# Two layers of cached attention and a token mixer on one core: a third PSUM bank keeps rows of V between the layers, and sums of heads go into the columns of x

## The chip, the cores and the metric

The kernel runs on one core of one Trainium2 chip. The metric is the time of one execution on the device in microseconds (us), as the median of several runs; the profile shows one execution, with its trace.

## What is computed

Two tokens (batch B = 2, one new position each) of width D = 512 pass four steps, each added to its input: attention over a cache, a token mixer, and both once more with the same weights and the same cache.

```python
x = x + _A_ref(_layernorm(x), k_cache, v_cache, wq, wo)   # layer 0
x = x + _B_ref(_layernorm(x), w1, b1, w2, b2)
x = x + _A_ref(_layernorm(x), k_cache, v_cache, wq, wo)   # layer 1
x = x + _B_ref(_layernorm(x), w1, b1, w2, b2)
# _A_ref: q = x @ wq, 32 query heads on 8 kv heads, Dh = 128, Sk = 32768 cached positions:
#   softmax(q k^T / sqrt(Dh)) v, then @ wo
# _B_ref: u = gelu(h * w1 + b1) over F = 1792 hidden values, then u @ w2 + b2, per channel
```

All is float32. [...]

## The kernel before

**Units and chunks.** A unit is one (layer, batch, kv head): 32 units in `units`. For each, K and then V are streamed in 8 chunks of 4096 positions; a chunk is 2 MiB, 4096 columns of 128 partitions. The big tile `mem` has 13 cells of one chunk each (cells 0 to 8 the ring, 9 to 12 for weights or more chunks, `WCELL0` = 9) and behind them a rest of 2560 columns, called cell 13 here. A load may fill half a cell: 6.0 and 6.5 are the halves of cell 6. The loads are issued by SyncE (`load`, L139; weights in `load_weights`, L118), in program order, and each waits until TensorE has read what its buffer held. Where a load goes is planned in Python (`spread`, `buffer`, `half`, `hold`, `room`), by the step at which each half cell becomes free.

**Work on a chunk.** `k_chunk` (L425) multiplies a K chunk with the queries, into a bank of scores. After all eight, `highest`, `max_1`, `max_2` (L440 to L456) find the maxima, `turn_scores` (L460) transposes the scores into the tiles `S0` and `S1` (half 0 is chunks 0 to 3, half 1 is 4 to 7), and `exponentials` (L465) runs on ScalarE. `v_chunk` (L578) then multiplies V chunks into the bank `acc`. `denominators` sums up. A unit's end is `out_0` (L546, L548: the four blocks of `acc` added), `out_1` (L618 to L620: turned and divided) and `out_2`, four products with `wo` that add the unit's row to the bank `rows` (`add_row`, L245). V of a unit runs while K of the next one is loaded. Queries of the coming unit come from `make_q` and `q_products` (L339).

**The order.** `parts` gives the loads of a unit as (first chunk, number of chunks). `stream` sorts all loads by a key; the constant `FOLLOWS` sets by hand the keys of V in the units N1 + 2 and N1 + 5. Every other step (`at(time, f, ...)`) is put at a step of that stream.

**The changes of layer.** Each batch's last unit of layer 0 is that of the keeper head 7: `N1` (the 14th unit) for batch 0, `N2` (three units on) for batch 1. The units around are: N1 = (layer 0, batch 0, head 7); (0, 1, 5); (1, 0, 7); N2 = (0, 1, 7); (1, 0, 5); N3 = (1, 1, 7); (1, 1, 5). After the last V chunk of N1 the row sums go through the mixer, which gives x of layer 1: `mix_1` (L640: x broadcast into the bank `bcast`), `out_0` to `out_2`, `take_rows` (L632, L633: copy `rows`, then clear the batch's row in it), `mix_2` (L664 on), `hidden_sum` (14 gelu steps, ScalarE L803 and VectorE L818, L820), `mix_3` (L828), `to_columns` (L311), and then the first queries of layer 1. Meanwhile K of the unit N1 + 1 is loaded in halves of a chunk (1 MiB).

**What stays.** K and V of the keeper head are the last of layer 0 and the first of layer 1, so part of them stays on the chip: `KEPT_K` names chunks of K, `KEPT` chunks of V with the number of quads that stay and their cell. A quad is 512 columns of 128 partitions, 256 KiB, as much as one PSUM bank. Of V chunk 4, five quads stay in cell 13; the other three are loaded into a half cell (6.0). Two of these three are copied into PSUM banks (`kept`, L537) and back into memory in layer 1 (L526); the third is loaded again:

```python
IN_PSUM = (4, 5, 2)          # chunk, quads that stay in memory, quads in PSUM
KEPT = {1: (8, 8), 2: (8, 9), 3: (8, 10), 4: (5, 13), 5: (8, 3), 6: (8, 4), 7: (8, 5)}
```

PSUM has eight banks: `scores` twice, `acc`, `kept0`, `kept1`, `rows`, `bcast`, `small`.

Of the kernel before, what the change touches and what calls it, by code (L numbers as in the profile page):

```python
# [26 lines left out]
RING_CELLS = 11  # L27
PLACE_V = {(1, 7): 1}
REST = 5
IN_PSUM = (4, 5, 2)  # L30
KEPT_Q = 4
RESIDENT = (5, 7)
TWO_HEADS = ((0, 1), (2, 3), (4, 6), RESIDENT)
FOLLOWS = {2: (2.2, -0.9, -0.8, -0.7, 3.5, -0.6, -0.5, -0.4), 5: (3.05, 1.1, 1.2, 1.3, 5.1, 3.1, 3.2, 3.3)}
PIECES = (32, 16, 8, 4, 4)
THIN = 16
QT = 4
# [7 lines left out]
def gqa_mixer_kernel(ctx: ExitStack, tc: tile.TileContext, x, kt, v, wqo, cols, out):  # L45
# [66 lines left out]
    def wo_at(h):  # L112
        return cells(home[h])[:, W:].rearrange("p (t c) -> p t c", t=R)
# [110 lines left out]
    kept = [pfix.tile([P, 512], F32, name=f"kept{k}") for k in range(IN_PSUM[2])]  # L224


    rows = pfix.tile([P, 512], F32, name="rows")
    nc.vector.memset(rows, 0.0)


# [9 lines left out]
        return small[:, turn[0] % NG * P :][:, :P]  # L240


    def add_row(g, b, weights, row):

        nc.tensor.matmul(  # L245
            rows[32 * g : 32 * g + b + 1, :],
            weights if b else weights[:, 1:],
            row,
            start=False,
            stop=True,  # L250
            skip_group_check=True,
        )
# [48 lines left out]
    def spot():  # L301

        spots[0] += 1
        return cells(RING * RING - 1)[:, spots[0] % (CK // D) * D :][:, :D]
# [27 lines left out]
    def q_products(n, *ds):  # L332

        layer, b, h = unit_of(n)
        m = 1 if partner(n) is None else B
        for d in ds:
            if d == 0:
                q_ps[n] = pfix.tile([P, 512], F32, name="bcast") if N1 < n <= N3 + 2 else kept[0]
            nc.tensor.matmul(  # L339
                q_ps[n][:m, :],  # L340
                xnT[:, d, b : b + m],
                wq_at(h)[:, d, :],
                start=(d == 0),
                stop=(d == DT - 1),
            )
# [147 lines left out]
    def load_v(n, c, m, limit):  # L493
        layer, b, h = unit_of(n)
        src = piece(v, b * HKV + h, c, m)
        stay, own = stays(n, c)
        until = v_done[n, c + m - 1]
        w = QT * DH
        f = stay * w
        at = quads(own) if stay else []  # L500
        if stay and m > 1:
            k = KEPT[c][1]
            own = cells(k, m)
            load(own, src)
            for j in range(m):
                hold(k + j, 1, v_done[units.index((1, b, h)), c + j])
                v_at[n, c + j] = quads(cells(k + j))
            return
        if stay:
            if layer == 0:  # L510
                load(own, src[:, :f])
                for j in range(2 if stay > QT else 1):
                    busy[2 * KEPT[c][1] + j] = v_done[units.index((1, b, h)), c]
            if stay == JT // QT:
                v_at[n, c] = at
                return
            bufs = [half(until)[:, : CK - f]]
        elif limit == RING:
            bufs = spread(m, until, False, PLACE_V.get((n - N1, c)))
        else:  # L520
            bufs = [buffer(m, limit, until)]
        rest = [q for t in bufs for q in quads(t)]
        banks = list(zip(kept, rest)) if (c, stay) == IN_PSUM[:2] and stay else []
        if layer:
            for k, quad in banks:
                nc.vector.tensor_copy(quad, k)  # L526
        last = n == NU - 1 and c + m == NCH
        for t in bufs:
            if layer and stay:
                f += len(banks) * w  # L530
                t = t[:, len(banks) * w :]
            for k in [k * DH for k in PIECES] if last else (t.shape[-1],):
                load(t[:, :k], src[:, f : f + k])
                f, t = f + k, t[:, k:]
        if not layer:
            for k, quad in banks:
                nc.vector.tensor_copy(k, quad)  # L537
        at = at + rest
        for j in range(m):
            v_at[n, c + j] = at[j * (JT // QT) : (j + 1) * (JT // QT)]  # L540
# [78 lines left out]
        oT[n] = oz[n % 2]  # L619
        nc.vector.tensor_mul(oT[n][:, :, 1], po[:, :R], rl[n])  # L620

    def out_2(n):
        layer, b, h = unit_of(n)
        for r in range(R):
            add_row(r, b, oT[n][:, r, :], wo_at(h)[:, r, :])

    ysb, px = {}, {}
    slope, shift, stats = {}, {}, {}

    def take_rows(key, y):  # L630
        ysb[key] = y if y is not None else spot()
        nc.vector.tensor_copy(ysb[key], rows)  # L632
        nc.vector.tensor_scalar_mul(rows, rows, others[:, key[1] : key[1] + 1])  # L633

    def mix_1(key):

        b = key[1]
        px[key] = pfix.tile([P, 512], F32, name="bcast")
        for d in range(DT):
            nc.tensor.matmul(  # L640
                px[key][:, d * P : (d + 1) * P],
                xT[b][:, d : d + 1].to_broadcast([P, P]),
                ident,
                start=(d == 0),
                stop=False,
                skip_group_check=True,
            )
# [31 lines left out]
    def last_rows(key):  # L679


        b = key[1]
        y = spot()
        nc.vector.tensor_copy(y, rows)
        nc.vector.memset(kept[0][:, :DH], 0.0)
        w = D // 2
        halves[0] = pfix.tile([P, 512], F32, name="bcast")
        halves[1] = pscore.tile([P, 512], F32, name="scores")
        for k in range(2):
            for d in range(DT // 2):  # L690
                nc.tensor.matmul(
                    halves[k][:, d * P : (d + 1) * P],
                    xT[b][:, k * DT // 2 + d : k * DT // 2 + d + 1].to_broadcast([P, P]),
                    ident,
                    start=(d == 0),
                    stop=False,
                    skip_group_check=True,
                )
            nc.tensor.matmul(
                halves[k][:, :w], sel[b], y[:, k * w : (k + 1) * w], start=False, stop=True, skip_group_check=True  # L700
            )
# [155 lines left out]
    def parts(n, with_v):  # L857
# [6 lines left out]
        if not with_v:  # L864
            loads = ((0, 3), (3, 1), (4, 2), (6, 2)) if n in (N1, N2) else ((0, 2), (2, 2), (4, 2), (6, 2))
            if n in (N1 + 1, N2 + 1):
                loads = ((0, 2), *((c, 1) for c in range(2, NCH)))
            if n in (N1 + 2, N3):
                loads = [(c, 1) for c in range(NCH)]
        elif n in (N1, N2):  # L870
            loads = ((0, 1), (5, 3), (1, 3), (4, 1))
        elif n in (N1 + 1, N2 + 1):
            loads = [(c, 1) for c in range(NCH)]
        elif n < N1:
            loads = ((0, 2), (2, 2), (4, 2), (6, 2))
        else:
            loads = [(c, 1) for c in range(NCH)]
# [38 lines left out]
    for n in range(NU):  # L916
# [60 lines left out]
        change = n in (N1, N2)  # L977
        at(vend if change else min(vend + 1, vbeg[n + 1]), out_0, n)
        at(vend + 0.5 if change else min(vend + 1, vbeg[n + 1]), out_1, n)
        at(vend + 1 if change else vend if n == NU - 2 else vend + 2, out_2, n)  # L980
        if units[n] == lay[layer, b][-1]:
            key = (layer, b)
            at(vend - 1 if change else vend, mix_1, key)
# [124 lines left out]
```

## Time and profile before

| | |
|---|---|
| time, median of 3 runs | 2496.51 us (2495.5 to 2499.65) |
| the profiled execution | 2498.0 us, its span 2496.2 us |
| bytes moved by DMA | 1063.04 MB, mean 426 GB/s |
| TensorE busy | 1374.8 us (55%), granted clock 0.77 on the mean |
| VectorE busy | 240.2 us (10%) |
| ScalarE busy | 187.4 us (8%) |

The chain that ended last is read backwards from the last instruction; an entry "DMA" in it is time from the issue of a load to its landing, an entry "PE" a stretch in which a product was what the next step waited for. A row of SyncE is the issue of a load, not its transfer. Times of a row are microseconds from the start of the span. First comes the start, then the length; in brackets stands how long the engine was idle before it and what ended that.

### The profile page before, as it was taken

What the parts mean: (1) busy time and instruction counts of PE and PEld (TensorE: products, weight loads), DVE (VectorE), ACT (ScalarE), POOL (GpSimd) and SP (SyncE); (2) the same over time, 40 slices, a digit from 0 to 9 for tenths busy, and PEclk for the clock granted to TensorE, in tenths of its full rate; (3) what the DMA queues carried; (4) which work ended last, traced back from release to release, by engine and by line L of the source; (5) the groups of instructions that cost most, each with busy time, mean ns of one, the idle gap of its engine ahead of it and who ended that gap; (6) DMA issues with size and microseconds to landing.
All of it is one profiled execution on the core that took longest, in us unless ns stands there. A gap on an engine that the chain in (4) does not pass through costs nothing.

```text
span 2496.2 us, 20457 instructions
## 1 busy us (share of the span) xinstructions
PE 1374.8 (55%) x9270; PEld 373.0 (15%) x9270; DVE 240.2 (10%) x632; ACT 187.4 (8%) x554; POOL 4.9 (0%) x17
## 2 busy tenths in 40 slices
PE   4545445645445544657677666465455464456546
PEld 1111111111111111111121111111111111111112
DVE  1000000000000000003113100000000000010002
ACT  0000000000000000002012000000000000011002
POOL 0000000000000000000000000000000000000000
PEclk8777767876777777778887887777778677777778
DMA  9999999999999999999999999999999999999996
GB/s 420 435 435 427 436 429 436 431 434 431 435 434 431 433 427 431 430 429 388 432 430 401 427 426 430 439 433 431 430 437 430 431 433 433 434 429 433 427 434 279
DMA packets 30336, 1063.04 MB, mean 426 GB/s; under 512 B 3621, under 2 KB 3625, under 8 KB 4522
## 3 DMA queue, kind: packets, MB, share of 16 engines
q1 hardware_dynamic: 29960, 1061.70, 99.0%
q8 instruction: 73, 1.20, 0.2%
q14 instruction: 13, 0.11, 0.0%
q10 hardware_dynamic: 290, 0.04, 0.0%
HBM read 1061.72 MB, written 0.00 MB: 425 GB/s over the span
## 4 chain that ended last, share of the span: by engine, by line
DMA 74%; PE 24%; another core or an unknown queue 0%; issue 0%; DVE 0%; ACT 0%; SPq 0%
DMA mem<-in_v_dram 63%; PE acc L578 19%; DMA mem<-in_kt_dram 12%; PE scores L425 3%; PE small L454 0%; PE small L609 0%; PE rows L245 0%; PE bcast L339 0%; PE small L448 0%; PE kept L760 0%; PE bcast L664 0%; PE bcast L640 0%; DVE S L548 0%; ACT S L465 0%
## 5 line engine op out<-in xcount | busy, mean ns | idle before, releaser
L425 PE MATMUL scores<-mem,small_sb 128*32 128x512 f32 x4096 | 634.8, 739 | 610.0 <-DMA mem<-in_kt_dram 609.9
L578 PE MATMUL acc<-mem,S 128*16 128x512 f32 x4088 | 601.4, 728 | 459.8 <-DMA mem<-in_v_dram 453.4
L425 PEld LDWEIGHTS scores<-mem,small_sb 128*32 128x32 f32 x4096 | 151.4, 129 | 999.2 <-issue 910.3
L465 ACT ACTIVATE S<-S,small_sb 128x128 f32<-128x128 f32 x240 | 123.3, 517 | 2105.5 <-DVE small_sb L456 1630.7
L578 PEld LDWEIGHTS acc<-mem,S 128*16 128x16 f32 x4088 | 133.1, 110 | 819.9 <-issue 694.1
L440 DVE TENSOR_REDUCE small_sb<-scores 128x1 f32<-128x512 f32 x64 | 44.2, 691 | 813.6 <-PE scores L425 813.6
L460 DVE STREAM_TRANSPOSE S<-scores 128x512 f32<-128x512 f32 x64 | 45.4, 710 | 114.6 <-PE acc L578 114.6
L339 PE MATMUL kept<-mem,small_sb 128*2 128x512 f32 x104 | 51.2, 618 | 1.7 <-DVE small_sb L273 1.7
L245 PE MATMUL rows<-mem,small_sb 128*1 128x512 f32 (+1 forms) x276 | 49.0, 605 | 2.6 <-ACT mem L803 2.4
L465 ACT ACTIVATION_READ_ACCUMULATOR S<-S,small_sb 128x1 f32 x240 | 44.8, 187 | 0.0
L611 DVE RECIPROCAL small_sb<-small 128x4 f32<-128x4 f32 x32 | 5.9, 184 | 322.9 <-PE small L609 322.9
L450 DVE TENSOR_REDUCE small_sb<-small 1x4 f32<-1x128 f32 x32 | 8.9, 279 | 277.7 <-PE small L448 277.7
L620 DVE TENSOR_TENSOR small_sb<-small,small_sb 128x4 f32<-128x4 f32 x31 | 5.1, 164 | 295.6 <-PE small L618 295.6
L548 DVE SCALAR_TENSOR_TENSOR S<-acc,small_sb,S 128x128 f32<-128x128 f32 x93 | 32.6, 351 | 3.3
L803 ACT ACTIVATE S<-bcast,small_sb 128x512 f32<-128x512 f32 x28 | 21.5, 777 | 95.4 <-DVE small_sb L672 93.3
L365 PE MATMUL small<-small_sb,mem 2*128 2x2 f32 x112 | 14.8, 250 | 17.9 <-DVE mem L361 17.9
L546 DVE TENSOR_SCALAR S<-acc,small_sb 128x128 f32<-128x128 f32 x31 | 10.8, 350 | 132.4 <-PE acc L578 132.4
L618 PEld LDWEIGHTS small<-small_sb,S 128*128 128x128 f32 x62 | 12.6, 254 | 48.5 <-issue 40.8
L339 PE MATMUL bcast<-mem,small_sb 128*1 128x512 f32 (+1 forms) x40 | 19.5, 603 | 0.0
L820 DVE SCALAR_TENSOR_TENSOR acc<-S,small_sb,acc 128x512 f32<-128x512 f32 x24 | 18.1, 755 | 2.5
L365 PEld LDWEIGHTS small<-small_sb,mem 2*128 2x128 f32 x112 | 13.7, 188 | 30.6 <-DVE mem L361 27.3
L448 PE MATMUL small<-small_sb 128*1 128x128 f32 x64 | 16.6, 353 | 1.5 <-DVE small_sb L446 1.3
(134 smaller groups left out, 267.3 us busy)
## 6 DMA issues: line engine op xcount, KB each, us to landing
mem<-in_kt_dram SPq DMA_DIRECT2D x14, 4096.0 KB, 24.8
mem<-in_v_dram SPq DMA_DIRECT2D x9, 4096.0 KB, 23.2
mem<-in_wqo_dram SPq DMA_DIRECT2D x7, 4096.0 KB, 37.6
mem<-in_kt_dram SPq DMA_DIRECT2D x12, 2048.0 KB, 21.0
mem<-in_v_dram SPq DMA_DIRECT2D x4, 6144.0 KB, 28.4
mem<-in_kt_dram SPq DMA_DIRECT2D x24, 1024.0 KB, 9.3
mem<-in_v_dram SPq DMA_DIRECT2D x11, 2048.0 KB, 20.2
mem<-in_v_dram SPq DMA_DIRECT2D x21, 1024.0 KB, 8.8
```

The costliest lines, as they stand in the source:

```text
L245: nc.tensor.matmul(rows[32 * g : 32 * g + b + 1, :], weights if b else weights[:, 1:], row, start=False, stop=True, skip_group_check=True,)
L339: nc.tensor.matmul(q_ps[n][:m, :], xnT[:, d, b : b + m], wq_at(h)[:, d, :], start=(d == 0), stop=(d == DT - 1),)
L365: nc.tensor.matmul(pt[:, r * m : (r + 1) * m], q_row[n][:m, r * DH : (r + 1) * DH], ident[:m, :m], start=True, stop=True,)
L425: nc.tensor.matmul(sc_ps[n, half][32 * g : 32 * g + 32, :], q, kc[k * NG + g], start=(i == 0 and k == 0), stop=(i == PACK - 1 and k == SUB ...
L440: nc.vector.tensor_reduce(mx[n][:, half : half + 1], sc_ps[n, half], axis=AX.X, op=ALU.max)
L448: nc.tensor.matmul(pm[:1, :P], mxa, ident, start=True, stop=True)
L460: nc.vector.transpose(S[half], sc_ps[n, half])
L465: nc.scalar.activation(s[:, :, h], s[:, :, h], AF.Exp, bias=neg[n][:, h : h + 1], scale=SCALE, accum_out=lsum[n][:, half, h : h + 1],)
L548: nc.vector.scalar_tensor_tensor(t, acc[:, k * DH : (k + 1) * DH], mask[:, k : k + 1], t, op0=ALU.mult, op1=ALU.add)
L578: nc.tensor.matmul(acc[32 * g : 32 * g + R * QT, :], S[half][:, col : col + R * QT], vc[q], start=(c == v_from[n] and q < NG), stop=(c == ...
L803: nc.scalar.activation(hid[key, f], px[key], AF.Gelu_apprx_tanh, bias=shift[key][:, f : f + 1], scale=slope[key][:, f : f + 1],)
L820: nc.vector.scalar_tensor_tensor(h if f == FT - 1 else acc, h, w, acc, op0=ALU.mult, op1=ALU.add)
```

## The change

- `IN_PSUM` goes from two banks to three. The third is the bank of `rows`, so all of chunk 4 of V stays, for both batches, and the loads of 512 columns in layer 1 go. From the load of that chunk at N1 until its last use at N3 the bank holds V.
- The row sums of the units before N1 are therefore taken out of the bank ahead of it (`fold_rows`, after the unit N1 - 1): copied to memory in the region of cell 13, multiplied with the selecting columns `selg` into columns, and added to x's columns `xcols`, which `mix_1` broadcasts later.
- Each of the units N1 + 1, N1 + 2 and N1 + 4 (those between N1 and N3 that are no change) puts its row into `bcast` instead (`row_to_fold`), copies it to a row tile, and adds it to x's columns one step later (`fold_row`).
- At the changes N1 and N2 themselves the unit's row goes into `acc`, and `take_rows` reads it there; nothing is cleared.
- At N3 the bank is set to zero after the quads are copied out, and holds row sums again.
- V of N1 and N2 is loaded as chunk 0, 1 to 3, 4, 5 and 6, 7, where it was 0, 5 to 7, 1 to 3, 4. `FOLLOWS[5]` puts V chunks 1 to 3 of N3 one step earlier, ahead of the first K of the next unit.

```diff
-IN_PSUM = (4, 5, 2)
+IN_PSUM = (4, 5, 3)
...
-FOLLOWS = {2: (2.2, -0.9, -0.8, -0.7, 3.5, -0.6, -0.5, -0.4), 5: (3.05, 1.1, 1.2, 1.3, 5.1, 3.1, 3.2, 3.3)}
+FOLLOWS = {2: (2.2, -0.9, -0.8, -0.7, 3.5, -0.6, -0.5, -0.4), 5: (3.05, 0.1, 0.2, 0.3, 5.1, 3.1, 3.2, 3.3)}
...
-    rows = pfix.tile([P, 512], F32, name="rows")
+    rows = kept[-1]
+    bcast = pfix.tile([P, 512], F32, name="bcast")
     nc.vector.memset(rows, 0.0)
...
-    def add_row(g, b, weights, row):
+    def add_row(g, b, weights, row, to=None):
         nc.tensor.matmul(
-            rows[32 * g : 32 * g + b + 1, :],
+            (rows if to is None else to)[32 * g : 32 * g + b + 1, :],
             weights if b else weights[:, 1:],
             row,
-            start=False,
+            start=to is not None,
...
         if layer:
             for k, quad in banks:
                 nc.vector.tensor_copy(quad, k)
+            if banks and n == N3:
+                nc.vector.memset(rows, 0.0)
...
+    def row_to_fold(n):
+        out_2(n, bcast)
+        folded[n] = row_tile()
+        nc.vector.tensor_copy(folded[n], bcast)
+
+    def fold(y, b, m):
+        pt = misc()
+        for d in range(DT):
+            nc.tensor.matmul(
+                pt[:, d * m : (d + 1) * m], y[:, d * P : (d + 1) * P], selg[:, b : b + m], start=True, stop=True
+            )
+        x = xcols[:, b : b + m, :]
+        nc.vector.tensor_add(x, x, pt[:, : DT * m].rearrange("p (d b) -> p b d", b=m))
+
+    def fold_row(n):
+        fold(folded.pop(n), unit_of(n)[1], 1)
+
+    def fold_rows():
+        y = mem[:, (WCELL0 + WCELLS) * CK :][:, :D]
+        nc.vector.tensor_copy(y, rows)
+        fold(y, 0, B)
...
     def take_rows(key, y):
         ysb[key] = y if y is not None else spot()
+        if key[0] == 0:
+            nc.vector.tensor_copy(ysb[key], acc)
+            return
         nc.vector.tensor_copy(ysb[key], rows)
         nc.vector.tensor_scalar_mul(rows, rows, others[:, key[1] : key[1] + 1])
...
         elif n in (N1, N2):
-            loads = ((0, 1), (5, 3), (1, 3), (4, 1))
+            loads = ((0, 1), (1, 3), (4, 1), (5, 2), (7, 1))
...
-        at(vend + 1 if change else vend if n == NU - 2 else vend + 2, out_2, n)
+        if N1 < n < N3 and not change:
+            at(vend + 2, row_to_fold, n)
+            at(vend + 3, fold_row, n)
+        else:
+            at(vend + 1 if change else vend if n == NU - 2 else vend + 2, out_2, n, acc if change else None)
+        if n == N1 - 1:
+            at(vend + 2, fold_rows)
```

More of the change, by code (lines that the diff above doesn't have):

```diff
@@ L337, in q_products @@
             if d == 0:
-                q_ps[n] = pfix.tile([P, 512], F32, name="bcast") if N1 < n <= N3 + 2 else kept[0]
+                q_ps[n] = bcast if N1 < n <= N3 + 2 else kept[0]
             nc.tensor.matmul(
@@ L531, in load_v @@
                 t = t[:, len(banks) * w :]
-            for k in [k * DH for k in PIECES] if last else (t.shape[-1],):
+            for k in [k * DH for k in PIECES] if last else (t.shape[-1],) if t.shape[-1] else ():
                 load(t[:, :k], src[:, f : f + k])
@@ L620, in out_1, with out_2 @@
         nc.vector.tensor_mul(oT[n][:, :, 1], po[:, :R], rl[n])
-    def out_2(n):
+    def out_2(n, to=None):
         layer, b, h = unit_of(n)
         for r in range(R):
-            add_row(r, b, oT[n][:, r, :], wo_at(h)[:, r, :])
+            add_row(r, b, oT[n][:, r, :], wo_at(h)[:, r, :], to)
+    folded = {}
+    def row_to_fold(n):
[16 more added lines that the diff above has]
+        fold(y, 0, B)
     ysb, px = {}, {}
@@ L637, in mix_1 @@
         b = key[1]
-        px[key] = pfix.tile([P, 512], F32, name="bcast")
+        px[key] = bcast
         for d in range(DT):
@@ L686, in last_rows @@
         w = D // 2
-        halves[0] = pfix.tile([P, 512], F32, name="bcast")
+        halves[0] = bcast
         halves[1] = pscore.tile([P, 512], F32, name="scores")
```

## The prediction

> **What bounds the kernel now.** I read the page first: span, DMA rows, chain.
>
> ```profile
> span 2496.2 us, 20457 instructions
> GB/s 420 435 435 427 436 429 436 431 434 431 435 434 431 433 427 431 430 429 388 432 430 401 427 426 430 439 433 431 430 437 430 431 433 433 434 429 433 427 434 279
> DMA packets 30336, 1063.04 MB, mean 426 GB/s; under 512 B 3621, under 2 KB 3625, under 8 KB 4522
> DMA 74%; PE 24%; another core or an unknown queue 0%; issue 0%; DVE 0%; ACT 0%; SPq 0%
> ```
>
> The loads set the time: some 430 GB/s in nearly every slice. Beside the end, two slices are low, 388 (the 19th) and 401 (the 22nd). They are the two changes of layer. Only bytes taken away, or gaps closed there, can shorten the span. Busy time by windows, cut to fit these gaps; columns are length, PE, PEld, DVE, ACT, POOL busy, PE clock, DMA share, GB/s:
>
> ```profile
> 1138.00:1154.00 16.00, 14.41 (x104) 4.09 (x100) 4.38 (x10) 0.00 (x0) 0.00 (x0) 0.88 0.89 355
> 1154.00:1164.00 10.00, 6.28 (x40) 0.81 (x32) 7.54 (x15) 7.07 (x10) 0.54 (x1) 0.75 1.00 378
> 1176.00:1194.00 18.00, 14.37 (x98) 3.91 (x97) 6.57 (x13) 1.26 (x2) 0.00 (x0) 0.98 1.01 392
> 1324.00:1345.00 21.00, 14.68 (x104) 4.20 (x108) 4.22 (x10) 0.00 (x0) 0.00 (x0) 0.84 0.94 385
> 1345.00:1354.00 9.00, 5.08 (x36) 0.89 (x37) 6.75 (x13) 6.07 (x8) 0.54 (x1) 0.79 0.99 368
> 1440.00:1460.00 20.00, 19.72 (x158) 5.46 (x162) 2.76 (x5) 0.00 (x0) 0.00 (x0) 0.86 0.97 406
> 1460.00:2440.00 980.00, 523.54 (x3448) 141.10 (x3444) 73.17 (x205) 68.98 (x213) 0.54 (x1) 0.75 1.00 433
> ```
>
> The last row is the rate with a full queue, 433. Against it the windows lose (1 - rate/433) x length: 2.9, 1.3 and 1.7 us around the first change (5.9), 2.3 and 1.4 around the second (3.7), 1.2 at 1440. These 10.8 us are all that can be won from gaps.
>
> What opened them: SyncE issues in program order, so one load that waits for its buffer holds all behind it. SyncE's own timeline (start, length, load):
>
> ```profile
> 1114.27 34.10 SPq L139 DMA_DIRECT2D mem<-in_kt_dram  x2
> 1304.24 35.29 SPq L139 DMA_DIRECT2D mem<-in_kt_dram  x2
> 1452.22 0.33 SPq L118 DMA_DIRECT2D mem<-in_wqo_dram  x1
> ```
>
> In the first two rows two half-chunk loads of K stand together: the first goes at 1114.27, the second at about 1148.04 (end 1148.37 less 0.33), and at 1339.20. The second writes the half cell (6.0) that holds the last quads of V chunk 4 of the keeper head; chunk 4 is computed last, so the load waits until TensorE is through with all of V. Three halves were queued ahead of it and had run out. In the third row the weights of the next two heads wait for cells 9 and 10, read by V chunks 2 and 3 of the second batch's keeper unit.
>
> **Bytes.** Two loads of 512 columns go (the last quad of chunk 4 in layer 1, for each batch).
>
> ```profile
> mem<-in_v_dram SPq DMA_DIRECT2D x4, 256.0 KB, 28.7
> mem<-in_kt_dram SPq DMA_DIRECT2D x24, 1024.0 KB, 9.3
> ```
>
> The first row has them, beside two of the tail's. 2 x 262,144 B at 433 GB/s are 1.2 us off. That chunks 5 to 7 go as two loads instead of one adds two issues, so the count of loads stays, and issues lie deep in the queue.
>
> **The first change, new order.** V comes as 0, 1-3, 4, 5-6, 7. Chunk 4 is then done early and half 6.0 is free long before V ends: four halves of K (2.4 us each: 1 MiB at 433 GB/s) are queued behind V, not three. The next load, into 6.5, waits for the first half chunk of K on TensorE. The old order there, in TensorE's timeline, and VectorE's rows that start when chunk 4 lands:
>
> ```profile
> 1137.55 7.50 PE L578 MATMUL acc<-mem,S 128*16 128x512 f32 x48 [6.24 <-DMA mem<-in_v_dram]
> 1144.98 1.16 PE L640 MATMUL bcast<-small_sb 128*128 128x128 f32 x8
> 1146.07 1.91 PE L578 MATMUL acc<-mem,S 128*16 128x512 f32 x16
> 1147.79 1.04 PE L425 MATMUL scores<-mem,small_sb 128*32 128x512 f32 x8
> 1314.28 3.62 PE L578 MATMUL acc<-mem,S 128*16 128x512 f32 x16 [12.36 <-DMA mem<-in_v_dram]
> 1328.73 7.48 PE L578 MATMUL acc<-mem,S 128*16 128x512 f32 x48 [6.25 <-DMA mem<-in_v_dram]
> 1337.23 1.91 PE L578 MATMUL acc<-mem,S 128*16 128x512 f32 x16
> 1142.66 1.29 DVE L537 COPY kept<-mem 128x512 f32<-128x512 f32 x2 [15.22 <-DMA mem<-in_v_dram]
> 1334.98 1.29 DVE L537 COPY kept<-mem 128x512 f32<-128x512 f32 x2 [16.35 <-DMA mem<-in_v_dram]
> ```
>
> Old: three chunks land together at 1137.55, TensorE runs 7.50, then the broadcasts 1.16, then chunk 4, 1.91: V ends at 1147.98 though all of it had landed at 1142.66. New: the last load is one chunk (2 MiB, 4.8 us) and lands at the same 1142.6; chunks 5-6 land 4.8 us before, at 1137.8, and take 3.62 (a chunk after a wait, at the slow clock: the row at 1314.28) plus 1.91, to 1143.3; broadcasts and chunk 7 end V at 1146.4. TensorE is 1.6 us earlier, the transfers are covered 2.4 us longer: 4.0 against a gap of 2.9, which closes here. How much survives is set by the chain behind V (13 gelu steps and more, all compute), whose end meets the last half of K:
>
> ```profile
> 1175.04 0.71 DVE L460 STREAM_TRANSPOSE S<-scores 128x512 f32<-128x512 f32 x1
> 1176.24 0.69 DVE L440 TENSOR_REDUCE small_sb<-scores 128x1 f32<-128x512 f32 x1 [0.50 <-PE scores L425]
> 1366.14 1.07 PE L425 MATMUL scores<-mem,small_sb 128*32 128x512 f32 x8 [0.43 <-DMA mem<-in_kt_dram]
> 1367.28 0.69 DVE L440 TENSOR_REDUCE small_sb<-scores 128x1 f32<-128x512 f32 x1 [0.50 <-PE scores L425]
> ```
>
> VectorE waits 0.5 us for K's last half there (TensorE 0.43 for its load), so it can come forward by TensorE's 1.6 and that 0.5: 2.1 us. I take **2.1**. The bounds are 0 (the whole gap comes back at the next V) and 5.9.
>
> **The second change.** There the old end is 1339.14 and the last byte at 1334.98. New: chunks 5-6 land between 1328.7 (old row's landing) and 1330.2 (4.8 us before 1335.0), plus 5.53, 1.16 and 1.91: 1337.3 to 1338.8 (the broadcasts wait for chunk 6, chunk 7 has landed). Lead 0.3 to 1.8, middle 0.8; with 0.4 of slack **1.2**; bounds 0 and 3.7.
>
> **Weights.** V chunks 1-3 of that unit are resident; moved ahead of the next unit's first K they no longer wait for its landing:
>
> ```profile
> 1440.21 6.35 PE L425 MATMUL scores<-mem,small_sb 128*32 128x512 f32 x32 [5.75 <-DMA mem<-in_kt_dram]
> 1446.38 3.62 PE L578 MATMUL acc<-mem,S 128*16 128x512 f32 x32
> 1450.24 1.91 PE L578 MATMUL acc<-mem,S 128*16 128x512 f32 x16
> 1438.84 0.16 DVE L608 TENSOR_TENSOR small_sb<-small_sb 128x4 f32<-128x4 f32 x1 [3.56 <-ACT S L465]
> ```
>
> The exponentials they need are through at 1438.84. Three chunks at 3.62 at the most end by 1449.7, at 1.9 by 1444.5, against 1452.15; the gap is 1.2 us. I take **1.1** (bounds 0 and 1.2).
>
> **Added work.** Four foldings (the old row sums before the first change, then three units): a copy of a bank, four products, an addition; two more bank copies each way, a memset. Prices and what covers them:
>
> ```profile
> 1151.92 0.69 DVE L632 COPY S<-rows 128x512 f32<-128x512 f32 x1 [1.72 <-PE rows L245]
> 1173.62 1.05 PE L311 MATMUL small<-small_sb,S 128*128 128x1 f32 x8
> 1112.00 25.51 DMA mem<-in_v_dram
> 1260.00:1280.00 20.00, 20.00 (x162) 6.15 (x154) 4.74 (x11) 0.00 (x0) 0.00 (x0) 1.00 1.02 435
> 1271.10 23.62 DMA mem<-in_kt_dram
> ```
>
> A fold is 0.69 + 1.05 and about 0.2 for the addition: 1.9 us, of which TensorE stands for the copy and its products. The first one also holds a load: V chunk 4 goes into the region that the sums are copied to, and all of V and K queue behind it on SyncE. The cover is the queue: in the chain of waits the 6 MiB of 1112.00 land 25.51 us later, 14.5 of these their own, so 11 us were queued ahead, and the same in the 4 MiB of 1271.10 (23.62 - 9.7: 14). TensorE is full from 1260 to 1280, and two folds (3.8 us) go before or into it; 14 us hold them. At the changes themselves the sums go into the accumulator bank, which is free by then: no wait, and one VectorE pass less, off the path. Cost taken 0, bounds 0 and 4 x 1.9 = 7.6.
>
> **Sum:** 1.2 + 2.1 + 1.2 + 1.1 = 5.6 us. The profiled execution took 2498.0 us with its span of 2496.2, so it would become 2492.4; it lies 1.5 above the median 2496.51 of three runs (2495.5 to 2499.65), so I forecast **2490.9**. 0.2%, about what a measurement of this kernel can tell from no change, is 5.0 us: below 2491.5 is faster.
>
> **Rivals.**
> *TensorE gains no lead.* A chunk after a wait runs slow, and a clock that stays low through both chunks 5 and 6 eats the lead.
>
> ```profile
> 1136.00:1140.00 4.00, 2.45 (x12) 0.48 (x16) 0.00 (x0) 0.00 (x0) 0.00 (x0) 0.50 0.95 396
> 1140.00:1144.00 4.00, 4.00 (x32) 0.94 (x28) 1.29 (x2) 0.00 (x0) 0.00 (x0) 0.76 1.02 418
> ```
>
> The granted clock was 0.50 just there, and rose within 1140 to 1144. Two chunks at 3.62 end V at 1148.1, as late as now. Then only the slack of 0.4 is won at each change, and the gap returns where the next V waits: 1.2 + 0.9 + 1.1 = 3.2, 2493.3. For it: the rows; against it: the old three chunks took 7.50, so the second ran fast. The Trainium skill (TensorE: Matmul & The Clock Gate, What's actually happening) states that an idle window of about 3.4 us halves the clock and a busy one restores it; by that rule the new wait before chunk 5 also costs the slow start, and a badly placed window gives this rival's time. The trace agrees with the halving: 0.50. Chance 0.25.
> *The later gaps shrink too* (all 5.9 at the first change rather than 2.1): 5.6 + 3.8 = 9.4, 2487.1. For it: halves land 9.3 us after issue, and four halves carry 9.7, so a small lead could keep them full. Against: the wait at 1176 ends on compute. Chance 0.12.
> *The folds lie open*: slower. If TensorE, full from 1260 to 1280, becomes the bound from the first change to the second, the gaps move instead of closing and the four folds add 7.6: 2496.5 - 1.2 + 7.6 = 2502.9. It decides once the queue at 1255 to 1300 holds less than 8 us; the rows say 14. Chance 0.07.
> That the change does not do what it says is excluded by the program as built: the two small loads are gone from it.
>
> **How the numbers follow.** Forecast 0.56 (its own range 2489.5 to 2492.5: the bounds of the second change's lead, and the spread of the runs), no lead 0.25, later gaps 0.12, folds open 0.07. The range leaves out the folds and the better half of the later gaps: 2487.5 to 2495.3, its top being the bytes alone. Faster: three quarters of the forecast and all of the later gaps but a little, 0.55; slower 0.07; same 0.38.
>
> **What would show it.** DMA bytes 1062.5 MB; the 19th and 22nd slices higher by some 15 and 8 GB/s; the first load after the four halves issued while the queue still runs, so the window from 1138 to 1154 back near 430 GB/s; the weights issued before about 1450. Wrong would be: SyncE waiting long for the load of chunk 4 on the fold's products, or a new low window between 1190 and 1324.

## The result, and the profile after

The changed kernel takes 2490.59 us (median of 9 runs, 2490.07 to 2496.12), beside 2497.07 for the kernel before on the same chip (9 runs, 2495.5 to 2499.66). The ratio is 0.9977, 95% interval 0.9968 to 0.9986: 6.5 us less by the medians (3.5 to 8.0 by the interval), 0.3 below the forecast of 2490.9. The profiled execution took 2490.09 us, 7.9 less than that of before, its span 8.2 less.

From the page of the changed kernel, the span, the rate in 40 slices and the DMA line:

```profile
span 2488.0 us, 20543 instructions
GB/s 421 437 432 428 433 436 430 434 435 427 436 436 432 426 436 431 427 431 407 433 427 417 428 432 432 438 430 431 432 428 438 428 429 435 431 434 431 432 431 291
DMA packets 30336, 1062.51 MB, mean 427 GB/s; under 512 B 3621, under 2 KB 3625, under 8 KB 4266
```

0.53 MB are gone. The 19th slice rose from 388 to 407, the 22nd from 401 to 417: they were forecast to rise by some 15 and 8, and rose by 19 and 16. The windows of the changed kernel, cut as before (the last column is GB/s):

```profile
1138.00:1154.00 16.00, 13.88 (x100) 3.89 (x92) 3.83 (x12) 0.00 (x0) 0.54 (x1) 0.89 0.98 389
1154.00:1164.00 10.00, 4.86 (x32) 0.70 (x32) 8.11 (x11) 9.07 (x12) 0.00 (x0) 0.90 0.98 401
1176.00:1194.00 18.00, 14.53 (x105) 4.12 (x106) 5.38 (x10) 1.26 (x2) 0.00 (x0) 0.91 1.01 413
1324.00:1345.00 21.00, 15.39 (x108) 4.20 (x108) 5.92 (x15) 2.88 (x4) 0.54 (x1) 0.92 0.99 414
1345.00:1354.00 9.00, 5.39 (x32) 0.72 (x32) 7.85 (x12) 8.16 (x12) 0.00 (x0) 0.77 1.01 421
1440.00:1460.00 20.00, 17.00 (x158) 4.63 (x150) 4.10 (x9) 2.19 (x8) 0.00 (x0) 0.98 1.02 434
```

As (1 - rate/433) x length, the first three rows lose 1.6, 0.7 and 0.8 us, where they lost 2.9, 1.3 and 1.7; the next two 0.9 and 0.2, where they lost 2.3 and 1.4; the last nothing, where it lost 1.2. By these rates the gaps are smaller at every one of the places, but the first window is at 389, not near 430, as if only half of the gap at the first change had closed.

The landings say more. The rate of a window counts the packets that start in it, while the next step waits for the landing of a whole load. TensorE's rows that wait for one half chunk of K after the other behind the first change, in the changed kernel and then before:

```profile
1154.95 1.06 PE L426 MATMUL scores<-mem,small_sb 128*32 128x512 f32 x8 [1.48 <-DMA mem<-in_kt_dram]
1157.39 1.06 PE L426 MATMUL scores<-mem,small_sb 128*32 128x512 f32 x8 [1.38 <-DMA mem<-in_kt_dram]
1159.84 1.06 PE L426 MATMUL scores<-mem,small_sb 128*32 128x512 f32 x8 [1.39 <-DMA mem<-in_kt_dram]
1162.33 1.94 PE L426 MATMUL scores<-mem,small_sb 128*32 128x512 f32 x8 [1.43 <-DMA mem<-in_kt_dram]
```

```profile
1158.64 1.63 PE L425 MATMUL scores<-mem,small_sb 128*32 128x512 f32 x8 [1.77 <-DMA mem<-in_kt_dram]
1161.71 1.94 PE L425 MATMUL scores<-mem,small_sb 128*32 128x512 f32 x8 [1.44 <-DMA mem<-in_kt_dram]
1165.16 1.93 PE L425 MATMUL scores<-mem,small_sb 128*32 128x512 f32 x8 [1.51 <-DMA mem<-in_kt_dram]
```

The halves come 2.4 to 2.5 us apart now, and came 3.07 and 3.45 us apart. From each issue and its time to landing in the trace: the twelve halves of K at the first change land between 1144.90 and 1172.23, in 27.3 us, which is eleven steps of 2.48; before they took 30.1, to 1175.06. So by the landings the stream runs at its pace through the first change, and the gap there is closed. At the second change the twelve halves take 27.3 us too.

SyncE's timeline of the changed kernel shows the mechanism at work, with the loads behind the four halves:

```profile
1114.66 32.39 SPq L139 DMA_DIRECT2D mem<-in_kt_dram  x3
1146.72 0.33 SPq L139 DMA_DIRECT2D mem<-in_kt_dram  x1
1148.88 0.33 SPq L139 DMA_DIRECT2D mem<-in_kt_dram  x1
1152.67 0.33 SPq L139 DMA_DIRECT2D mem<-in_kt_dram  x1
1442.88 0.33 SPq L118 DMA_DIRECT2D mem<-in_wqo_dram  x1
```

The first row holds three loads: into 7.5, into 6.0 at 1132.84, long before V ends, and into 6.5, the one at 1146.72. This first load that waits for TensorE at the end of V goes 1.3 us earlier than the first waiting load of before (1148.04), and with one half more queued ahead of it: the half in front of it lands 5.6 us after its issue (1152.33), where it was 1.9 us before (1149.91). The weights go at 1442.88 instead of 1452.22.

### The profile page after: what moved, and what is told of

Same layout as the page of the kernel before. It is cut to its first block, busy times and chain, and to the rows that moved or that the text cites. A ratio compares the mean times of both kernels' runs of the same rounds, so it can differ in the third digit from the quotient of the medians.

```text
span 2488.0 us, 20543 instructions
## 1 busy us (share of the span) xinstructions
PE 1371.4 (55%) x9302; PEld 376.2 (15%) x9302; DVE 244.9 (10%) x643; ACT 187.7 (8%) x554; POOL 4.9 (0%) x17
## 4 chain that ended last, share of the span: by engine, by line
DMA 73%; PE 25%; DVE 1%; issue 0%; another core or an unknown queue 0%; ACT 0%; SPq 0%; POOL 0%; ACTq 0%
DMA mem<-in_v_dram 64%; PE acc L581 20%; DMA mem<-in_kt_dram 9%; PE scores L426 3%; PE small L612 0%; PE small L455 0%; PE small L449 0%; PE bcast L340 0%; ACT S L466 0%; PE small L642 0%; PE kept L246 0%; PE kept L792 0%; PE bcast L672 0%; DVE S L551 0%
## 5 line engine op out<-in xcount | busy, mean ns | idle before, releaser
L246 PE MATMUL kept<-mem,small_sb 128*1 128x512 f32 (+1 forms) x236 | 42.4, 598 | 2.6 <-ACT mem L835 2.4
L366 PEld LDWEIGHTS small<-small_sb,mem 2*128 2x128 f32 x112 | 14.3, 196 | 30.5 <-DVE mem L362 27.3
```

Source lines behind the costliest of these rows:

```text
L246: nc.tensor.matmul((rows if to is None else to)[32 * g : 32 * g + b + 1, :], weights if b else weights[:, 1:], row, start=to is not None, ...
L366: nc.tensor.matmul(pt[:, r * m : (r + 1) * m], q_row[n][:m, r * DH : (r + 1) * DH], ident[:m, :m], start=True, stop=True,)
```

## The experiments

All medians in one table, each with its ratio to the kernel before beside it on the same chip, and the rate in three stretches of its profiled execution (around the first change, around the second, around the weights):

| kernel | median us | ratio, 95% interval | 1138 to 1200 | 1310 to 1400 | 1400 to 1480 |
|---|---|---|---|---|---|
| before | 2496.9 to 2498.0 | | 389 | 409 | 425 |
| after | 2490.59 | 0.9977 (0.9968 to 0.9986) | 408 | 422 | 431 |
| after_again | 2491.83 | 0.9977 (0.9967 to 0.9988) | 408 | 422 | 432 |
| order_only | 2493.33 | 0.9980 (0.9971 to 0.9989) | 399 | 404 | 427 |
| follows_only | 2496.47 | 0.9998 (0.9989 to 1.0006) | 402 | 408 | 431 |
| bank_only | 2498.05 | 1.0002 (0.9993 to 1.0010) | 398 | 402 | 412 |
| reload_quad | 2492.15 | 0.9980 (0.9971 to 0.9988) | 404 | 417 | 429 |
| no_row_folds | 2491.54 | 0.9979 (0.9970 to 0.9987) | 398 | 419 | 431 |
| folds_longer | 2495.95 | 0.9998 (0.9989 to 1.0007) | 409 | 420 | 425 |
| first_only | 2493.92 | 0.9988 (0.9979 to 0.9996) | 408 | 405 | 431 |
| singles_mix | 2490.79 | 0.9974 (0.9965 to 0.9983) | 407 | 423 | 423 |
| mix_in_wait | 2491.55 | 0.9973 (0.9963 to 0.9984) | 405 | 422 | 432 |
| k_half_first | 2490.49 | 0.9973 (0.9962 to 0.9983) | 406 | 421 | 430 |
| both_steps | 2490.97 | 0.9972 (0.9961 to 0.9984) | 408 | 422 | 429 |

The two measurements of the changed kernel differ by 1.2 us; smaller differences are not read as effects.

**The parts alone.** `order_only` is the kernel before with nothing but the new order of V:

```diff
-            loads = ((0, 1), (5, 3), (1, 3), (4, 1))
+            loads = ((0, 1), (1, 3), (4, 1), (5, 2), (7, 1))
```

> The kernel before with the new order of V's loads at the two changes alone (0, 1-3, 4, 5-6, 7); two banks, the old row sums, the old FOLLOWS. Theory (the order closes the two gaps, independently of the rest): 3.3 us under the kernel before, some 4 if later gaps shrink as in the profile after; V of the first change ends near 1146 us of the span where it was 1148.0, and the half load that waited until 1148.04 goes near 1133. Rival (the gap moves to the next V): at most 1 us under. Rival (the freed bank and the bytes carry it): no change.

V of the first change ended at 1145.64 and the half load went at 1132.38, as expected. By the medians this line alone is worth 4.6 us (2.7 to 7.2 by the interval) of the 6.5; the prediction's terms for it were 2.1 + 1.2. In its profiled execution the gain at the second change is missing (404, no better than before). Its windows there:

```profile
1324.00:1345.00 21.00, 14.75 (x102) 4.09 (x103) 4.49 (x13) 0.54 (x1) 0.54 (x1) 0.84 0.98 408
1362.00:1366.00 4.00, 4.00 (x21) 2.05 (x18) 1.08 (x4) 0.00 (x0) 0.00 (x0) 0.57 1.02 412
1366.00:1370.00 4.00, 4.00 (x9) 0.83 (x8) 1.11 (x4) 0.00 (x0) 0.00 (x0) 0.57 0.96 369
1368.00:1384.00 16.00, 14.96 (x107) 4.07 (x104) 5.72 (x11) 1.26 (x2) 0.00 (x0) 0.96 0.84 335
```

The gap did shrink first (408 against 385) and then opened at the next V (335, where the kernel before had 418). Two things stand ahead of it in the trace: a half of K that landed 1.5 us late (1361.31), and a granted clock of 0.57 from 1362 to 1370, in TensorE's work between the last K and that V. This execution took 2496.14, the slowest of its eleven. So a whole gap can come back at the next V, the lower bound of the prediction's term, but it did so in one execution, and which of the two did it is not shown.

`follows_only` is the kernel before with the new `FOLLOWS[5]`, `bank_only` the changed kernel with the old order and the old `FOLLOWS[5]`:

```diff
-... 5: (3.05, 1.1, 1.2, 1.3, 5.1, 3.1, 3.2, 3.3)}
+... 5: (3.05, 0.1, 0.2, 0.3, 5.1, 3.1, 3.2, 3.3)}
```

> The kernel before with the new FOLLOWS alone: V chunks 1 to 3 of N3 ahead of the next unit's first K. Theory: the weights are issued 8 to 10 us earlier than 1452.2, the window from 1440 to 1460 goes from 406 to some 430 GB/s, and the time falls by 1.1 us. Rival (the queue is made up behind it anyway): no change in time, within 0.3.

> The changed kernel with the old order of V's loads and the old FOLLOWS: what is left is the third bank, the folds and 0.52 MB fewer bytes. Theory (folds hidden): 1.2 us under the kernel before, the two gaps at the changes and that of the weights as before. Rival (folds partly open): 0 to 3 us above that, that is up to 2 us slower than before. Rival (the bank carries it): 5 us or more under.

When the weights go in `follows_only`; and in `bank_only`, with a fold's products, the V chunks behind them and the window around:

```profile
1443.22 0.33 SPq L118 DMA_DIRECT2D mem<-in_wqo_dram  x1
```

```profile
1443.82 1.87 PE L642 MATMUL small<-small_sb,S 128*128 128x1 f32 x8
1448.86 3.61 PE L581 MATMUL acc<-mem,S 128*16 128x512 f32 x32
1454.68 0.33 SPq L118 DMA_DIRECT2D mem<-in_wqo_dram  x1
1440.00:1460.00 20.00, 19.75 (x142) 6.38 (x146) 1.99 (x6) 2.14 (x8) 0.00 (x0) 0.78 0.84 343
```

The constant does alone what it was forecast to do to the load (1452.22 becomes 1443.22) and gains some 1.5 us in the median, with an interval that takes in no change: forecast (1.1) and rival (nothing) are not told apart. The bank alone gains nothing, though it moves 1.2 us less: TensorE is full there (19.75 of 20 us), the third row fold (1.87 at 1443.82) stands ahead of V chunks that the weights wait for, the weights go 2.5 us later than before, and the window loses 4.2 us instead of 1.2. So at this place the folds look free only with the new `FOLLOWS[5]`; this is read from one execution of `bank_only`, and no run takes the folds out of it. The terms "bytes", "weights" and "folds" of the sum were priced as independent, and by this reading they are not.

`reload_quad` is the changed kernel with the 512-column loads back (two kept quads, one loaded again):

```diff
-        banks = list(zip(kept, rest)) if (c, stay) == IN_PSUM[:2] and stay else []
+        banks = list(zip(kept[:2], rest)) if (c, stay) == IN_PSUM[:2] and stay else []
```

> The changed kernel with two quads kept in banks, so the third of chunk 4 is loaded again in layer 1, for both batches (0.52 MB more); folds, order and FOLLOWS as in the changed kernel. Theory: 1.2 us slower than the changed kernel, that is some 5.3 us under the kernel before, since each load queues behind others. Rival (a small load also holds its fixed time, as it has its own issue and landing): 4 to 5 us slower than the changed kernel. Rival (bytes are free): no difference to the changed kernel.

0.3 to 1.6 us above the two measurements of the changed kernel: it fits the 1.2 us of the bytes and can't say more.

**The folds.** `no_row_folds` takes the products and the addition of the three row folds away, `folds_longer` does all products four times:

```diff
     def fold(y, b, m):
+        if m == 1:
+            return
```

> The changed kernel, without the products and the addition that bring the rows of the units N1 + 1, N1 + 2 and N1 + 4 into x's columns (so these rows are missing from x of layer 1); the rows' products and their copies stay, and fold_rows stays. Compared with the changed kernel at 2490.6. Theory of the prediction (the queue covers the folds, cost 0): 2490.6, within 0.5. Rival (folds lie open, TensorE is the bound between the changes): three times 1.25 to 2.07 us less (1.05 to 1.87 of products, 0.2 of addition), so 2484.4 to 2486.9. Third reading, from the depth of the queue in the trace after (the load of K chunks 4 and 5 of the unit N2 goes out at 1256.11 with 2.4 us still queued, the weights at 1442.88 with 3.0): no time now, but that depth rises to some 4.5 and 4.5, so 2490 to 2490.6 here.

```diff
-        for d in range(DT):
+        for d in 4 * list(range(DT)):
```

> The changed kernel, with the products of each of the four folds done four times (same result): 3.15 us more TensorE per fold at full clock. Theory of the prediction (11 to 14 us of queue in front of the folds): 2490.6, no change. Rival from the depth of the queue in the trace after: the fold at 1110.84 is covered (6.7 us queued behind it), the one at 1283 too (over 6), but the load at 1256.11 with 2.4 us queued and the weights at 1442.88 with 3.0 run dry, and a single load needs some 2 us from its issue before bytes come at full rate: 2 to 3 us at the first and about 2 at the second, so 2494.5 to 2495.5. If folds lay open wholly: 4 x 3.15 = 12.6 more, 2503.

Without the folds (rows of three units are then missing from x of layer 1) nothing is gained: 2491.54, between the two measurements of the changed kernel. Longer folds cost 4.1 to 5.4 us. Where, in TensorE's and SyncE's timelines and the windows of `folds_longer`:

```profile
1248.55 6.99 PE L642 MATMUL small<-small_sb,S 128*128 128x1 f32 x32
1261.55 0.33 SPq L139 DMA_DIRECT2D mem<-in_kt_dram  x1
1449.90 0.33 SPq L118 DMA_DIRECT2D mem<-in_wqo_dram  x1
1250.00:1270.00 20.00, 20.00 (x140) 9.27 (x144) 1.18 (x5) 2.13 (x8) 0.00 (x0) 0.74 0.89 364
1440.00:1460.00 20.00, 20.00 (x166) 8.31 (x165) 2.88 (x7) 2.14 (x8) 0.00 (x0) 0.88 0.96 396
```

and the same places in the changed kernel:

```profile
1248.87 1.87 PE L642 MATMUL small<-small_sb,S 128*128 128x1 f32 x8
1256.11 0.33 SPq L139 DMA_DIRECT2D mem<-in_kt_dram  x1
1250.00:1270.00 20.00, 20.00 (x160) 5.80 (x161) 1.19 (x5) 2.14 (x8) 0.00 (x0) 0.89 1.03 437
```

The fold takes 6.99 instead of 1.87 (the granted clock is 0.50 from 1248 to 1256), the load of K chunks 4 and 5 of N2 goes 5.4 us later, and the window falls from 437 to 364: 3.2 us; the weights' window loses 1.7. The other two folds cost nothing even so (1138 to 1200 at 409, 1310 to 1400 at 420). So the cover is a matter of each place. The cover of a load is the time from its issue until the load ahead of it has landed. The expectations put 2.4 us at 1256.11 and 3.0 at 1442.88; by the landings it is 5.9 (to 1262.04) and 7.0 (to 1449.90) in the changed kernel, and 10.4 at the former place before (from 1255.22 to 1265.58). Of the 4.4 us that are gone, 2.9 are the stream's gain itself, which brings the loads ahead of it forward while TensorE stays where it was, 0.6 the small load that stood there, and 0.9 the later issue. In `folds_longer` 0.5 us were left at 1261.55, and that load landed 3.0 us late.

**The second change.** `first_only` keeps the old order at N2:

```diff
-        elif n in (N1, N2):
+        elif n == N1:
             loads = ((0, 1), (1, 3), (4, 1), (5, 2), (7, 1))
+        elif n == N2:
+            loads = ((0, 1), (5, 3), (1, 3), (4, 1))
```

> The changed kernel with the new order of V at the first change alone; N2 loads V as before (0, 5 to 7, 1 to 3, 4). Prediction's terms: 1.2 us slower than the changed kernel, 2491.8. By the bytes missing in the windows of the two traces (4.5 us lost between 1310 and 1400 before, 2.5 after): 2.0, so 2492.6. Rival (what the first change gains is given back at the second, where TensorE has not come forward by as much): the whole gain of the order is lost, 2495. In the trace: the windows 1324 to 1345 and 1345 to 1354 back at some 385 and 370 GB/s, 1138 to 1154 still near 390.

Its windows around the second change:

```profile
1324.00:1345.00 21.00, 17.18 (x124) 4.63 (x124) 6.34 (x16) 1.44 (x2) 0.54 (x1) 0.88 0.99 391
1345.00:1354.00 9.00, 5.81 (x24) 0.60 (x24) 7.85 (x12) 8.03 (x11) 0.00 (x0) 0.55 0.96 397
```

2.1 to 3.3 us slower than the changed kernel by the medians (the intervals of the two ratios overlap), with the gap back at the second change and the first change as good as there (408). The order is worth some 2 to 3 us at the second change, not the 1.2 taken, and the first change keeps its gain without the second. The landings agree wherever a trace has the first and the last of the twelve halves: with the old order they take 29.4 (`follows_only`, first change), 29.5 (`first_only`, second) and 30.6 us (`bank_only`, second), with the new one 27.3 to 27.8.

**More lead.** If TensorE's lead at the change closes the gap, more lead closes more of it. `singles_mix` loads chunks 5 and 6 singly and puts the broadcasts of `mix_1` one step earlier:

```diff
-            loads = ((0, 1), (1, 3), (4, 1), (5, 2), (7, 1))
+            loads = ((0, 1), (1, 3), (4, 1), (5, 1), (6, 1), (7, 1))
...
-            at(vend - 1 if change else vend, mix_1, key)
+            at(vend - 2 if change else vend, mix_1, key)
```

> The changed kernel with V chunks 5 and 6 of N1 and N2 as two loads, and the broadcasts of mix_1 one step earlier, ahead of these chunks, where TensorE sits idle 4.8 us for them. V should end when chunk 7 has landed and is computed: 1144.4 to 1144.7 at N1 where it is 1145.8 now, and 1.1 to 1.4 earlier at N2 too. Theory (TensorE's lead at the change is the term that closes the gap, microsecond for microsecond): 1.2 at each change, 2488.2; the window 1138 to 1154 rises from 389 to some 415. Rival 1 (the lead of the first change is eaten by the load at 1256, which has 2.4 us of queue left): 2489.4. Rival 2 (the gap that is left comes from K's halves, of which too few are queued at a time, whatever V does): 2490.6, and the window stays near 390.

TensorE's timeline of `singles_mix`, and of the changed kernel the three rows that stand for the same work:

```profile
1134.48 1.16 PE L672 MATMUL bcast<-small_sb 128*128 128x128 f32 x8
1137.53 1.91 PE L581 MATMUL acc<-mem,S 128*16 128x512 f32 x16 [1.89 <-DMA mem<-in_v_dram]
1142.45 3.62 PE L581 MATMUL acc<-mem,S 128*16 128x512 f32 x16 [3.01 <-DMA mem<-in_v_dram]
```

```profile
1137.55 5.32 PE L581 MATMUL acc<-mem,S 128*16 128x512 f32 x32 [4.79 <-DMA mem<-in_v_dram]
1142.81 1.16 PE L672 MATMUL bcast<-small_sb 128*128 128x128 f32 x8
1143.89 1.91 PE L581 MATMUL acc<-mem,S 128*16 128x512 f32 x16
```

The lead was not there. Everything but chunk 7 is done early, so TensorE waits 3.01 us for it and then computes it at half the clock (granted 0.50 from 1142 to 1146): 3.62 instead of 1.91. V ends at 1146.07, not at the 1144.4 expected and no earlier than the 1145.80 of the changed kernel, where the broadcasts keep TensorE running until chunk 7 has landed. The window 1138 to 1154 came to 374, not 415. The expectation left out what the prediction's first rival was about.

`mix_in_wait` leaves chunks 5 and 6 together and moves the broadcasts into the wait ahead of them; `k_half_first` computes one half chunk of K ahead of the product of `mix_2`; `both_steps` is both; `after_again` the changed kernel beside them.

```diff
-            at(vend - 1 if change else vend, mix_1, key)
+            at(vend - 3 if change else vend, mix_1, key)        # mix_in_wait
...
-            at(vend + (1 if change else 3), mix_2, key)
+            at(vend + (1.5 if change else 3), mix_2, key)       # k_half_first
...
-                at(vend + 1, hidden_sum, key)
+                at(vend + 1.5, hidden_sum, key)                 # k_half_first
```

> The changed kernel itself once more, beside the three below on the same chip: 2490.6, within 0.7. In its trace the end of V at the first change at 1145.8, the load after the four halves issued at 1146.7, and 2.4 to 3 us lost in the windows 1138 to 1154, 1154 to 1164 and 1176 to 1194.

> The changed kernel with the broadcasts of mix_1 two steps earlier at both changes, into the 4.8 us in which TensorE waits for V chunks 5 and 6; chunks 5 and 6 stay one load, so chunk 7 follows them without a wait and at full clock. V should end 1.0 to 1.1 us earlier (1144.8 at N1, 1332.6 at N2), and the first load after the four halves with it. Theory (the lead of TensorE and of the chain behind V is worth its own length): about 1 us at each change, 2488.6. Rival 1 (the lead of the first change is lost at the load at 1256, which has 2.4 us of queue): 2489.6. Rival 2 (what is left of the gap doesn't hang on V's end): 2490.6, and the three windows unchanged.

> The changed kernel with one half chunk of K (the first half of chunk 3 of the next unit, landed at 1145.4) computed ahead of the product of mix_2, which waits 0.8 us for VectorE, where it comes behind it now. The load into 7.5, issued at 1152.67 now, should go at about 1150.5, and the one into 6.0 1 us earlier; the chain behind V starts some 0.2 us later. Theory of the prediction (the chain of compute behind V sets what survives): the bytes come earlier in the windows 1138 to 1164 and are missing in 1176 to 1194, time 2490.6 to 2491. Rival (the issue of the halves sets it): up to 1.5 us less at each change, 2487.6 to 2489.

> Both: the broadcasts in the wait and the half chunk of K ahead of mix_2. Theory (chain sets it): as the broadcasts alone, 2488.6 to 2488.8. If the issue of the halves sets it: 2486 to 2487.5. If neither: 2490.6.

All four lie within 1.4 us of each other, and none is measurably below the changed kernel; `after_again` itself came out 1.2 us above 2490.6, outside the 0.7 expected. The lead was there this time, in TensorE's timeline of `mix_in_wait`:

```profile
1137.47 7.04 PE L581 MATMUL acc<-mem,S 128*16 128x512 f32 x48 [3.49 <-DMA mem<-in_v_dram]
1147.34 1.07 PE L426 MATMUL scores<-mem,small_sb 128*32 128x512 f32 x8 [0.81 <-DMA mem<-in_kt_dram]
1167.46 1.93 PE L426 MATMUL scores<-mem,small_sb 128*32 128x512 f32 x8 [0.56 <-DMA mem<-in_kt_dram]
```

V ends at 1144.5, 1.3 us earlier. Then TensorE waits 0.81 us for the landing of the second half of K, ahead of the row's products in its order; the half after these starts at 1151.14, 0.4 earlier than in the changed kernel; and the tenth half of K at 1167.46, 0.2 later. The lead ends in a wait for a transfer. In `k_half_first` the load into 7.5 went at 1151.66 instead of 1152.67, with the same rate over the stretch. That a larger lead is worth nothing is what these runs show, and the landings say why: the twelve halves take 27.3 to 27.8 us in all four, at both changes, so they already come at the pace of the stream, and no gap is left there for a lead to close.

## Why the prediction was right, point by point

*The loads bind, and only bytes or gaps at the changes count.* Right in the main, by the table; how loosely the rates of one execution and the median go together shows `no_row_folds` (398 in its first stretch, median 2491.54).

*Bytes, 1.2.* 0.53 MB less, as said; the time of it fits `reload_quad`. But the bank that saves them gives them back at the weights when the order and the constant are left as they were.

*The first change, new order.* V was to end at 1146.4 and ended at 1145.80 in the row above (chunks 5 and 6 in 5.32, 5.53 expected): this part of the working is right to 0.6 us. "4.0 against a gap of 2.9, which closes here" is right by the landings: before, the halves fell behind their pace of 2.48 us by 0.8, 1.0 and 1.0 us (up to 1153.19, 1161.67 and 1167.61), 2.8 in all, and now they keep it. The sign named for it failed: the window was to be near 430 and is at 389. These are the changed kernel's windows behind the four halves:

```profile
1146.00:1148.00 2.00, 1.23 (x14) 0.45 (x10) 1.42 (x5) 0.00 (x0) 0.00 (x0) 1.00 0.88 307
1150.00:1152.00 2.00, 1.51 (x7) 0.46 (x10) 0.78 (x2) 0.00 (x0) 0.00 (x0) 1.00 1.00 365
1154.00:1156.00 2.00, 1.05 (x8) 0.18 (x8) 1.05 (x2) 1.81 (x3) 0.00 (x0) 1.00 0.87 315
```

Fewer packets start in these windows, but no half lands late. What shrinks is the time from the start of a half's last packet to its landing: 3.3 us for the half that lands at 1149.85, 1.6 for the one at 1162.29 (packets counted in order). So a low window alone does not show a gap in what TensorE gets, and the losses that prediction and text take from windows, here and at the other places, are estimates.

*How much survives.* Taken as 2.1, with the reason that a chain of compute meets the last K half. 2.8 us survived, by the windows and by the landing of the last half (1172.23 for 1175.06), and the reason was wrong, in both kernels. TensorE and VectorE of the changed kernel:

```profile
1167.30 1.83 PE L426 MATMUL scores<-mem,small_sb 128*32 128x512 f32 x8 [0.55 <-DMA mem<-in_kt_dram]
1169.07 1.12 PE L860 MATMUL bcast<-S,small_sb 128*128 128x512 f32 x2
1166.02 0.75 DVE L852 SCALAR_TENSOR_TENSOR S<-S,small_sb,acc 128x512 f32<-128x512 f32 x1
```

The last gelu step ends at 1166.77, and its product (L860) starts at 1169.07, right behind a K half that had waited for its transfer. The mixer had 2.3 us in hand; before, it was 2.2 (1168.93 to 1171.13, behind a half that had waited 0.65 us). So the halves of K end last, and what is won ahead of them is kept: V of the next unit starts at 1177.53 instead of 1180.37, 2.8 us earlier. Behind that, one late landing is left: a half of V comes 1.3 us late at 1188.46, though it was issued 5.2 us before the one ahead of it landed. A packet of the queue that the page calls "instruction" (16 KB, 1.1 us) starts at 1185.86, and another at 1403.84, ahead of a landing that is 1.2 us late at 1405.97; that these packets hold up the landings is a guess that no run tests.

*The second change, 1.2.* The lead was taken as 0.3 to 1.8, its "middle" as 0.8, which by these bounds would be 1.05; it came out at 2.1:

```profile
1325.40 5.32 PE L581 MATMUL acc<-mem,S 128*16 128x512 f32 x32 [4.89 <-DMA mem<-in_v_dram]
1331.75 1.91 PE L581 MATMUL acc<-mem,S 128*16 128x512 f32 x16
```

As many bytes of V have landed 3.3 us earlier than before (1325.40 against 1328.73), and V ends at 1333.66, 5.5 us earlier than 1339.14. This is the term that was mis-sized: it measured 2.1 to 3.3 by `first_only`, 2.5 by the windows.

*Weights, 1.1.* Issued at 1442.88, before the 1449.7 at most; the window went to 434. In time, `follows_only` does not tell the term from none.

*Folds, cost 0.* The number is right, the reason only by luck of size. Not 11 to 14 us of queue stood in front of the load that matters but 5.9, taken in the same way: the chain's rows that were read (1112.00 and 1271.10) are from the kernel before and, at the second place, of a load behind the one that the fold holds up, and the gain of the change itself uses up a part of the cover. The rival "folds lie open" was to decide below 8 us of queue; at 5.9 it did not. `folds_longer` left 0.5, and the gap opened.

*"TensorE gains no lead"* didn't come about here, and its mechanism is real: the two chunks after the wait took 5.32 us in the changed kernel, 5.75 in `after_again` and 6.53 in `k_half_first`, which is 1.2 us of V's end in programs that are the same up to these products:

```profile
1137.72 5.75 PE L581 MATMUL acc<-mem,S 128*16 128x512 f32 x32 [4.65 <-DMA mem<-in_v_dram]
```

```profile
1137.41 6.53 PE L581 MATMUL acc<-mem,S 128*16 128x512 f32 x32 [5.48 <-DMA mem<-in_v_dram]
```

The Trainium skill (TensorE: Matmul & The Clock Gate, What's actually happening) says that the window which measures activity runs freely, so that the point of the change of clock depends on where the first product falls in it; the three rows fit that, with 5.32 to 6.53 us, though the waits ahead of them differ too (4.65 to 5.48 us) and no run shows the window itself.

The sum, term by term: bytes 1.2 (1.2), first change 2.8 (2.1), second 2.5 (1.2), weights 1.2 (1.1), folds 0 (0): 7.7 by the windows of one execution against 5.6, and 6.5 by the medians. That the forecast came within 0.3 us is partly luck: the sum was 0.9 us short, and the time of the kernel before that it started from (2496.51) was 0.6 below the one measured beside the changed kernel (2497.07).

## What to carry to other kernels

Where a ring of buffers holds up a stream of loads, order the work so that the buffer which the next load needs is free first; one line did some two thirds of this change. Judge whether a gap has closed by when the loads land, not by the rate of a window alone, and once they land at an even pace look for no more gain in that place. Take the cover of an added step at the very load which that step holds up: a stream that is made faster uses up the cover of every step that doesn't move with it. Work put into a wait can make the engine idle, and slow, just before the piece that ends last.

## What the runs showed of the hardware

- The rate of a short window and the pace of the landings can part: 307 to 401 GB/s in the 2 us windows from 1146 to 1156 of the changed kernel, while halves of 1 MiB landed every 2.48 us.
- How much cover a load needs is not settled here: 0.5 us cost 3.0 us (`folds_longer`) and 1.9 cost 0.8 (before, at 1148.04); 4.7 and more cost the halves of K nothing at the first change of the changed kernel, but a half of V with 5.2 still came 1.3 late there, and in the kernel before a half of K with 3.8 came 0.6 late.
- The same 16 products took 1.91 us behind other work and 3.62 behind a wait of 3.01 us (`singles_mix`), so an earlier start was worth nothing.
- In one execution (`order_only`) the granted clock was 0.57 for 8 us, in TensorE's work ahead of loads that then went late, some 3 us against the kernel before by the windows. A late landing stood ahead of it too, so the clock's share is open.
